# Six cross layers on one core: product 3 of layers 0 to 4 by seven half-size products, and state sums by accumulating DMAs

## The chip, the core and the metric

The kernel runs on one core of one Trainium2 chip. TensorE (PE) multiplies, ScalarE (ACT) brings results from PSUM to SBUF, VectorE (DVE) does elementwise work, SyncE (SP) issues DMAs, GpSimd (POOL) is nearly unused. The metric is device time in microseconds, the median of several runs. One execution is taken by the profiler.

## The reference

The input has 16384 rows of 1024 columns; there are six layers with a 1024 x 1024 weight and a bias each, all in bfloat16.

```python
x = x0
for l in range(L):
    proj = jnp.einsum('bd,de->be', x, ws[l]) + bs[l]
    x = x0 * proj + x
return x
```

## The kernel before, in words

**Tiling.** Rows are worked in 16 pairs of two blocks of 512 (`NB`). Everything is held transposed, features on the 128 partitions: `x0T` and the state `xst` of a pair are tiles of 128 x (2 blocks n) x (8 feature slices) x 512; four slices make a half (`half(eh)`). Pairs go in 8 groups of two (loop `s`, pairs "A" and "B"); within a group the loop runs over layers l = 0 to 5 and in each over A and B. One pass is a **step**: 96 steps, A and B alternating, so that the elementwise end of one pair's layer lies in the other pair's step. Such an end is `trail(Y)`, run in the order that the list `order` gives.

**Products.** The two blocks and the two feature halves make a 2 x 2 matrix of blocks; a layer is one Strassen-Winograd round of seven products of 512 x 512 weights on 512 columns, numbered 1 to 7. A direct product is 16 matmuls 128x128 on 512 columns (`mm`). From the second step on product 2, and in the groups after the first also product 4, is done by a second round of seven products of 256 x 256 on 256 columns (`inner`, four matmuls each, 28 in all). In layer 0 of those groups (`in3`) product 3 is too. Its inputs are differences in `ti3` (k02, k1, k3), its result is in part accumulated in PSUM with product 5 (`S53`) and in part evicted to `E3`, `e6` and added by VectorE; `ti4` and `E4`, `e5` do the same for product 4, `ti2` and `ea`, `eb` for product 2.

**VectorE in a step.** T13 (differences T[5], T[7]), then of the other pair's trail: m1 (sum times x0), s11 (`C2` plus `P5s`), a1 (plus the state); T2, T4; s4, e4 (E4 into C2); i02, i1, i3 (inputs of product 4); mC2 and aC2 (both feature slices of the second half times x0, plus the state); then `EA` and `P1s` of the own pair, j02, j1, j3 (inputs of the next step's product 2), m0 and a0 (the first quarter of the own state), and `S53` plus `U2s`. Each is in program order (`pin`). All T tiles and evicted tiles (`U2s`, `P1s`, `S53`, `ea`, `e4`) have one buffer, `C2` (name "cb") has two.

**Weights.** The combined weights are computed in group 0 (`combo`) and stored to DRAM (`Lc`). Later groups load nine tiles of 512 KB a layer through a ring of nine (`RING`); `prefetch_upto` issues these loads on SP in the steps of pair B, each once its buffer is free. The third inner weights (`w3i`, in the buffer `P2s`) are loaded for layer 0 only.

**Inputs and outputs.** `bring("A")` and `bring("B")` load the next group's inputs by two transposing DMAs each, in layers 2 and 3 of A's steps (`pending` holds them until the weights of the step are asked for). A pair that has ended is turned by a DMA transpose (`turn_pair`) and written (`write_pair`) during the next group's layer 0.

Line names in the profile: L46 is `vtt`, L52 `acopy`, L55 `abias`, L419 `mm`, L427 `inner`, L99 `prefetch_upto`, L221 the input load, L325 and L332 `turn_pair` and `write_pair`.

Of the kernel before, what the change touches and what calls it, by code (L numbers as in the profile page):

```python
# [8 lines left out]
ADD = mybir.AluOpType.add  # L9
# [8 lines left out]
def kernel(  # L18
# [26 lines left out]
    def vtt(out, in0, in1, op):  # L45
        return pin(nc.vector.tensor_tensor(out=out, in0=in0, in1=in1, op=op))  # L46

    def vcopy(out, in_):
        return pin(nc.vector.tensor_copy(out=out, in_=in_))

# [6 lines left out]
    def pool(name, bufs, **kw):  # L57
        return ctx.enter_context(tc.tile_pool(name=name, bufs=bufs, **kw))
# [2 lines left out]
    dram = pool("dram", 1, space=bass.MemoryType.DRAM)  # L61
    big = pool("big", 1)
    t_pool, ti_pool, ei_pool = pool("tp", 1), pool("tip", 1), pool("eip", 1)
    ev_pool, cb_pool, wring = pool("evp", 1), pool("cbp", 2), pool("wring", RING)
    ps = [pool(f"ps{i}", KH, space=bass.MemoryType.PSUM) for i in range(2)]

    def wtile():
# [5 lines left out]
    def evt(name):  # L73
        return ev_pool.tile([P, KH, NB], BF16, name=name)
# [88 lines left out]
    def sub_w(w, h):  # L163
        return {(i, j): w[:, 2 * i:2 * i + 2, j * h:(j + 1) * h] for i in range(2) for j in range(2)}
# [91 lines left out]
    def trail(Y, store):  # L256

        if Y is None:
            return [None] * 7
        C2, E4, e5 = Y.C2, Y.E4, Y.e5  # L260
        eh1 = lambda t: t[:, :, KH:KD, :]
        m1, a1 = fin_of(Y, Y.C12, 0, 1)
        if Y.E3 is not None:
            def m1(E3=Y.E3, e6=Y.e6, C=Y.C12, mul=m1):
                for i in range(2):
                    vtt(E3[:, 2 * i:2 * i + 2, NQ:NB], E3[:, 2 * i:2 * i + 2, (1 - i) * NQ:(2 - i) * NQ], e6[:], ADD)
                vtt(C, C, E3, ADD)
                mul()

        def s4():  # L270
            for i in range(2):
                vtt(E4[:, 2 * i:2 * i + 2, NQ:NB], E4[:, 2 * i:2 * i + 2, (1 - i) * NQ:(2 - i) * NQ], e5[:], ADD)

        def a1s():
            if a1 is not None:
                a1()
            if store:
                store_half(Y, 0)

        return [m1, lambda: vtt(C2[:, 1], C2[:, 1], Y.P5s[:], ADD), a1s,  # L280
                s4 if E4 is not None else None,
                (lambda: vtt(C2[:, 0], C2[:, 0], E4[:], ADD)) if E4 is not None else None,
                lambda: vtt(eh1(Y.xst) if Y.l == 0 else C2[:], C2[:], eh1(Y.x0T), MULT),
                None if Y.l == 0 else (lambda: vtt(eh1(Y.xst), C2[:], eh1(Y.src_in), ADD))]

    def fin_of(Y, C, eh, n):
        xs = half(eh)
        if Y.l == 0:
            return [lambda: vtt(Y.xst[:, n, xs, :], C, Y.x0T[:, n, xs, :], MULT), None]
        return [lambda: vtt(C, C, Y.x0T[:, n, xs, :], MULT),  # L290
                lambda: vtt(Y.xst[:, n, xs, :], C, Y.src_in[:, n, xs, :], ADD)]

# [35 lines left out]
    def write_pair(Y):  # L328
        with nc.allow_non_contiguous_dma(reason="256B runs"):
            for n in range(2):  # L330
                r0 = Y.pr * PR + n * NB
                pin(nc.sync.dma_start(out[r0:r0 + NB, :].rearrange("(j p) (k r) -> p k j r", p=P, r=P),  # L332
                                      Y.x0T[:, n].rearrange("p k (j r) -> p k j r", r=P)))

    for s in range(NPAIR // 2):
        for l in range(L):
            for side in ("A", "B"):
                X, Y = cur[side], prev
                first, last = step == 0, (X.pr, l) == LAST
                in2, in4 = not first, s > 0 and not (s + 1 == NPAIR // 2 and l + 1 == L)  # L340
                X.l, in3 = l, l == 0 and s > 0
                psA, psX = ps[step % 2], ps[1 - step % 2]
                step += 1
                bias = lambda eh, m, l=l: b_all[:, l * KD + eh * KH + m: l * KD + eh * KH + m + 1]
# [5 lines left out]
                def bring(who, s=s, home=home):  # L350
                    pr = 2 * (s + 1) + (who == "B")
                    new[who] = Pair(pr, bigt(home["n" + who]))
                    load_x0(pr, new[who].x0T)

                if side == "B" and s + 1 < NPAIR // 2 and l == L - 1:
                    w3i = evt("P2s")
                    pending.insert(0, lambda w=w3i: pin(nc.sync.dma_start(w[:], lc(0, 10))))
                if side == "A" and s + 1 < NPAIR // 2:
                    if l == (2 if s > 0 else L - 1):
                        pending.append(lambda: bring("A"))  # L360
                    if l == 3 and s > 0:
                        pending.append(lambda: bring("B"))

                if s + 1 == NPAIR // 2 and side == "A" and l == 2:
                    x0R = bigt(home["nA"])[:].rearrange("p n k b -> p (n k b)").rearrange("p (j d) -> p j d", d=D)
# [66 lines left out]
                def evi(dst, pt):  # L432
                    acopy(dst, pt[:].rearrange("p (m b) -> p m b", m=2))
# [20 lines left out]
                ev(P1s, pA, 0, 0)  # L454
                t2, t4 = (None, None) if first else (X.T2, X.T4)
                i02, i1, i3 = inner_t(X, lambda: X.T[4], "ti4") if in4 else [None] * 3
                X.E3 = None
                k02, k1, k3 = [None] * 3
                if in3:
                    ti3 = X.xst[:, 0, KH:KD, :].rearrange("p q (k b) -> p q k b", k=2)  # L460
                    k02, k1, k3 = inner_t(X, lambda: X.rhs(3), "ti3", ti3)
                order = (m1, s11, a1, t2, k02, s4, k1, t4, k3, e4, i02, mC2, i1, aC2, i3)
                if in3 and side == "B":
                    order = (m1, s11, a1, t2, s4, t4, e4, k02, i02, k1, k3, mC2, i1, aC2, i3)
                for f in order:
                    if f is not None:
                        f()
                if in2:
# [47 lines left out]
                    end_of(Y, False)  # L516
                    w3 = weights(3)
                    if in3:
                        wk, wr3 = w3i[:].rearrange("p k (j e) -> p k j e", e=HE), sub_w(w3, HE)
                        b3, t3 = sub4(X.rhs(3)), X.ti3  # L520
                        colx = lambda m0, j, pX=pX: (lambda m: pX[m0 + m][:, j * NQ:(j + 1) * NQ])
                        inner(colx(0, 0), wr3[1, 0], b3[1, 0], False)
                        inner(colx(0, 1), wk[:, 2], b3[1, 1], False)
                        ev(S53, pX, 0, 0)
                        mm(5, w5, pX, 3, True)
                        ev(P5s, pX, 3)
                        ev(S53, pX, 1, 0)
                        ev(P1s, pA, 3, 0)
                    else:
                        mm(3, w3, pX, 0, False)  # L530
                        mm(5, w5, pX, 3, True)
# [66 lines left out]
                if s == 0:  # L598
                    if side == "A":
                        if l > 0 and l + 1 < L:  # L600
                            alloc(l + 1)
                        if l + 1 < L:
                            load_raw(l + 1, nc.sync, (12, 4, 1, 2) if l > 0 else (12,))
                        for pid in ((5, 6, 3) if 0 < l < L - 1 else ()):
                            combo(l + 1, pid)
                        if l in (0, L - 1):
                            combo(l, 9)
                    elif l + 1 < L:
                        for pid in (5, 6, 3) if l == 0 else ():
                            combo(1, pid)  # L610
                        combo(l + 1, 7)
                        combo(l + 1, 8)
                        if l == 0:
                            combo(0, 10)
                w6 = weights(6)
                end_of(Y, True)
                if last:
# [5 lines left out]
                if in4:  # L623
# [12 lines left out]
                    ev(U2s, pA, 0)  # L636
                    if in3:
                        y1, y5 = bank(psX), bank(psX)
                        X.E3 = X.xst[:, 1, 0:KH, :]
                        X.e6 = ei_pool.tile([P, 2, NQ], BF16, name="e6")  # L640
                        e3 = sub4(X.E3)
                    inner(cols(z1), wr4[0, 0], b4[0, 0], True)
# [22 lines left out]
                    inner(cols(z1), wj[:, 3], t4[:, 2], False)  # L665
                    evi(e4[1, 0], z1)
                    for m in range(1, KH):
                        mm(7, w7, pA, m, False)
                        ev(C2[:, 1], pA, m, 1)
                        if in3 and m == 1:  # L670
                            inner(cols(y1), wk[:, 3], t3[:, 2], False)
                            evi(e3[1, 0], y1)
# [13 lines left out]
                else:  # L686
# [11 lines left out]
                if s == 0 and side == "B" and 0 < l < L - 1:  # L698
                    combo(l, 9)
                if not last:  # L700
                    vtt(S53[:], U2s[:], S53[:], ADD)
                if late:
                    for f in (j02, j1, j3):
                        if f is not None:
                            f()
# [49 lines left out]
```

## Time and profile before

| | us |
|---|---|
| median of 3 runs | 2262.93 (2262.43 to 2262.95) |
| the profiled execution | 2263.38 |
| its span, first to last instruction | 2261.6 |
| a step of group 0 (layers 1 to 5) | 23.78 |
| a step of later groups, layers 1 to 5 | 23.38 |
| a step of later groups, layer 0, A and B | 22.98 and 23.07 |

The granted clock of TensorE is 1.0 throughout. Steps are windows between the first matmuls of product 1. Instructions on VectorE overlap a little: their durations add up to more than the time that they take in a row, so spacing from start to start is what is added.

### The profile page before, as it was taken

What the parts mean: (1) busy time and instruction counts of PE and PEld (TensorE: products, weight loads), DVE (VectorE), ACT (ScalarE), POOL (GpSimd) and SP (SyncE); (2) the same over time, 40 slices, a digit from 0 to 9 for tenths busy, and PEclk for the clock granted to TensorE, in tenths of its full rate; (3) what the DMA queues carried; (4) which work ended last, traced back from release to release, by engine and by line L of the source; (5) the groups of instructions that cost most, each with busy time, mean ns of one, the idle gap of its engine ahead of it and who ended that gap; (6) DMA issues with size and microseconds to landing.
All of it is one profiled execution on the core that took longest, in us unless ns stands there. A gap on an engine that the chain in (4) does not pass through costs nothing.

```text
span 2261.6 us, 33979 instructions
## 1 busy us (share of the span) xinstructions
PE 2253.6 (100%) x13093; PEld 1279.8 (57%) x13093; DVE 2140.2 (95%) x2444; ACT 1930.2 (85%) x3363; POOL 1.6 (0%) x10
## 2 busy tenths in 40 slices
PE   9999999999999999999999999999999999999999
PEld 4555555555655556555565555655556555565554
DVE  7999989999999999999999999999999999999999
ACT  6777788888988889888898888988889888898887
POOL 0000000000000000000000000000000000000000
PEclk9999999999999999999999999999999999999999
DMA  8423595623945249543494434944348443483337
GB/s 235 156 94 121 152 212 168 148 85 125 254 136 138 89 135 250 138 127 95 137 263 122 122 110 135 250 121 121 123 132 240 121 131 122 132 231 122 104 120 177
DMA packets 509606, 338.82 MB, mean 150 GB/s; under 512 B 390658, under 2 KB 470532, under 8 KB 509444
## 3 DMA queue, kind: packets, MB, share of 16 engines
q1 hardware_dynamic: 509444, 336.65, 53.5%
q8 instruction: 103, 1.69, 0.3%
q14 instruction: 59, 0.48, 0.1%
HBM read 217.59 MB, written 52.95 MB: 120 GB/s over the span
## 4 chain that ended last, share of the span: by engine, by line
PE 99%; DMA 0%; DVE 0%; SPq 0%; issue 0%; ACT 0%; DVEq 0%
PE px L419 72%; PE px L427 26%; PE px L414 1%; DMA wp<-in_ws_dram 0%; DVE cb L46 0%; SPq L120 0%; DVE eb L46 0%; DVE T L46 0%; SPq L210 0%; PE px L411 0%; PE px L409 0%; DVE wp L46 0%; ACT cb L52 0%; SPq L213 0%; DVEq L46 0%
## 5 line engine op out<-in xcount | busy, mean ns | idle before, releaser
L419 PE MATMUL px<-T,wp 128*128 128x512 bf16 x4384 | 1071.7, 379 | 0.0
L419 PEld LDWEIGHTS <-wp 128*128 128x128 bf16 x7120 | 696.5, 98 | 637.4 <-issue 0.7
L419 PE MATMUL px<-big,wp 128*128 128x512 bf16 x2736 | 659.3, 379 | 0.4 <-ACT big L52 0.4
L427 PEld LDWEIGHTS <-wp 128*128 128x128 bf16 x4920 | 480.8, 98 | 257.4 <-DVE big L46 2.8
L55 ACT ACTIVATE cb<-px,b_all 128x512 bf16<-128x512 f32 x760 | 504.5, 689 | 78.4 <-PE px L419 64.9
L427 PE MATMUL px<-ti,wp 128*128 128x256 bf16 x2684 | 402.6, 273 | 0.0
L52 ACT CAST ea<-px 128x512 bf16<-128x512 f32 x344 | 201.7, 586 | 133.5 <-PE px L427 133.5
L46 DVE TENSOR_TENSOR T<-big 128x4096 bf16<-128x4096 bf16 (+1 forms) x97 | 220.1, 2269 | 77.9 <-PE px L419 77.2
L52 ACT CAST U2s<-px 128x512 bf16<-128x512 f32 x384 | 229.2, 597 | 55.2 <-PE px L419 52.7
L55 ACT ACTIVATE P1s<-px,b_all 128x512 bf16<-128x512 f32 x380 | 254.2, 694 | 5.7 <-PE px L419 4.2
L55 ACT ACTIVATE S<-px,b_all 128x512 bf16<-128x512 f32 x380 | 244.1, 703 | 0.8 <-PE px L419 0.8
L46 DVE TENSOR_TENSOR T<-big,T 128x2048 bf16<-128x2048 bf16 x192 | 233.9, 1218 | 1.2
L52 ACT CAST P5s<-px 128x512 bf16<-128x512 f32 x384 | 219.5, 596 | 17.3 <-PE px L419 16.1
L46 DVE TENSOR_TENSOR big<-cb,big 128x4096 bf16<-128x4096 bf16 x95 | 217.0, 2284 | 0.4
L52 ACT CAST e<-px 128x512 bf16<-128x512 f32 x342 | 204.4, 606 | 0.0
L427 PE MATMUL px<-big,wp 128*128 128x256 bf16 x1252 | 187.9, 273 | 0.0
L46 DVE TENSOR_TENSOR cb<-cb,big 128x4096 bf16<-128x4096 bf16 (+2 forms) x89 | 184.9, 2080 | 0.7 <-ACT cb L52 0.5
L52 ACT CAST eb<-px 128x512 bf16<-128x512 f32 x258 | 152.2, 590 | 6.2
L427 PE MATMUL px<-T,wp 128*128 128x256 bf16 x984 | 134.2, 273 | 0.0
L46 DVE TENSOR_TENSOR S<-U2s,S 128x2048 bf16<-128x2048 bf16 (+1 forms) x97 | 117.1, 1207 | 3.1 <-ACT U2s L52 3.0
L46 DVE TENSOR_TENSOR cb<-cb,P5s 128x2048 bf16<-128x2048 bf16 (+1 forms) x97 | 117.1, 1208 | 0.1
L46 DVE TENSOR_TENSOR P1s<-P1s,big 128x2048 bf16<-128x2048 bf16 x90 | 109.7, 1219 | 7.9 <-ACT P1s L55 7.8
(81 smaller groups left out, 1475.7 us busy)
## 6 DMA issues: line engine op xcount, KB each, us to landing
wp<-Lc SPq DMA_DIRECT2D x252, 512.0 KB, 4.7
wp<-in_ws_dram SPq DMA_DIRECT2D x144, 512.0 KB, 3.7
out_dram<-big SPq DMA_DIRECT2D x28, 1024.0 KB, 11.0
Lc<-big SPq DMA_DIRECT2D x15, 512.0 KB, 2.7
Lc<-wp SPq DMA_DIRECT2D x9, 512.0 KB, 2.7
Lc<-ti SPq DMA_DIRECT2D x7, 512.0 KB, 3.7
P2s<-Lc SPq DMA_DIRECT2D x7, 512.0 KB, 4.6
ea<-in_ws_dram SPq DMA_DIRECT2D x6, 512.0 KB, 5.0
```

The lines of the kernel that those rows point to most:

```text
L46: return pin(nc.vector.tensor_tensor(out=out, in0=in0, in1=in1, op=op))
L52: return pin(nc.scalar.copy(out=out, in_=in_))
L55: return pin(nc.scalar.activation(out=out, in_=in_, func=IDENT, bias=bias, scale=1.0))
L414: nc.tensor.matmul(pt, lhsT=rhs[:, k, m * P:(m + 1) * P], rhs=wt[:, k, :], start=(start and k == 0 and pid != 1), stop=(k == KH - 1), **kw)
L419: nc.tensor.matmul(pts[m][:], lhsT=wt[:, k, m * P:(m + 1) * P], rhs=rhs[:, k, :], start=(start and k == 0), stop=(k == KH - 1), **kw)
L427: nc.tensor.matmul(dst(m), lhsT=w[:, k, m * P:(m + 1) * P], rhs=rhs[:, k, :], start=(start and m == 0 and k == 0), stop=(k == 1), skip_gro ...
```

## The change

- `in3` holds in layers 0 to 4 of the groups after the first: product 3 by seven products there. `E3` and `ti3` get tiles of their own. The third weights are loaded once a layer (`load_third`, in B's step for the next layer), and `combo` stores them for layers 0 to 4.
- `by_dma(Y)` holds in layers 1 to 4 of pair A and 1 to 3 of pair B. There three of the four state sums become accumulating DMAs on GpSimd's queue (`dadd`, state += product): m1d from `U2s`, m2d from `C2[:, 1]`, m0 from a tile in the one buffer of T2. The fourth stays on VectorE. The DMAs write into the state in place.
- The E3 corrections and S53 += E3 move from the next step's m1 to the end of the own step; mC2 stands before i02.
- `C2` has one buffer.
- Both inputs of the next group are loaded in layer 5 of A.
- In group 0 combo 9 stands in A's steps and combo 10 in B's.

```diff
+    def dadd(out, in_):
+        pin(nc.gpsimd.dma_start(out=out, in_=in_, accum_op=ADD))
...
-    ev_pool, cb_pool, wring = pool("evp", 1), pool("cbp", 2), pool("wring", RING)
+    ev_pool, cb_pool, wring = pool("evp", 1), pool("cbp", 1), pool("wring", RING)
...
+        mul = lambda n: vtt(C2[:, n], C2[:, n], Y.x0T[:, n, KH:KD, :], MULT)
+        def m1d():
+            vtt(Y.U2s[:], Y.C12, Y.x0T[:, 1, 0:KH, :], MULT)
+            dadd(Y.xst[:, 1, 0:KH, :], Y.U2s[:])
+        def m2d():
+            mul(1)
+            dadd(Y.xst[:, 1, KH:KD, :], C2[:, 1])
+        if dma:
+            return [m1d, s11, m2d, s4, e4, lambda: mul(0),
+                    lambda: vtt(Y.xst[:, 0, KH:KD, :], Y.xst[:, 0, KH:KD, :], C2[:, 0], ADD)]
...
+    def by_dma(Y):
+        return 0 < Y.l < L - 1 - Y.pr % 2
...
+        if by_dma(Y):
+            def m0():
+                t = t_pool.tile([P, KH, NB], BF16, name="T2")
+                vtt(t[:], C, Y.x0T[:, n, xs, :], MULT)
+                dadd(Y.xst[:, n, xs, :], t[:])
+            return [m0, None]
...
+    def load_third(l):
+        third[l] = evt("P2s")
+        pin(nc.sync.dma_start(third[l][:], lc(l, 10)))
...
-                X.l, in3 = l, l == 0 and s > 0
+                X.l, in3 = l, s > 0 and l < L - 1
...
-                    if l == (2 if s > 0 else L - 1):
+                    if l == L - 1:
                         pending.append(lambda: bring("A"))
-                    if l == 3 and s > 0:
-                        pending.append(lambda: bring("B"))
+                        if s > 0:
+                            pending.append(lambda: bring("B"))
...
-                order = (m1, s11, a1, t2, k02, s4, k1, t4, k3, e4, i02, mC2, i1, aC2, i3)
-                if in3 and side == "B":
-                    order = (m1, s11, a1, t2, s4, t4, e4, k02, i02, k1, k3, mC2, i1, aC2, i3)
+                order = (m1, s11, a1, t2, s4, t4, e4, k02, k1, k3, mC2, i02, i1, i3, aC2) if in3 else (m1, s11, a1, t2, s4, t4, e4, i02, mC2, i1, aC2, i3)
...
+                        if side == "B" and l + 1 < L - 1:
+                            load_third(l + 1)
...
+                if in3:
+                    for i in range(2):
+                        vtt(X.E3[:, 2 * i:2 * i + 2, NQ:NB], X.E3[:, 2 * i:2 * i + 2, (1 - i) * NQ:(2 - i) * NQ], X.e6[:], ADD)
+                    vtt(S53[:], S53[:], X.E3[:], ADD)
```

More of the change, by code (lines that the diff above doesn't have):

```diff
@@ L261, in trail @@
         eh1 = lambda t: t[:, :, KH:KD, :]
[L262 to L268, printed above, removed]
+        dma = by_dma(Y)
+        mul = lambda n: vtt(C2[:, n], C2[:, n], Y.x0T[:, n, KH:KD, :], MULT)
         def s4():
@@ L272, in s4 @@
                 vtt(E4[:, 2 * i:2 * i + 2, NQ:NB], E4[:, 2 * i:2 * i + 2, (1 - i) * NQ:(2 - i) * NQ], e5[:], ADD)
+        def m1d():
[4 more added lines that the diff above has]
+            dadd(Y.xst[:, 1, KH:KD, :], C2[:, 1])
+        s11 = lambda: vtt(C2[:, 1], C2[:, 1], Y.P5s[:], ADD)
+        e4 = (lambda: vtt(C2[:, 0], C2[:, 0], E4[:], ADD)) if E4 is not None else None
+        if E4 is None:
+            s4 = None
+        if dma:
+            return [m1d, s11, m2d, s4, e4, lambda: mul(0),
+                    lambda: vtt(Y.xst[:, 0, KH:KD, :], Y.xst[:, 0, KH:KD, :], C2[:, 0], ADD)]
+        m1, a1 = fin_of(Y, Y.C12, 0, 1)
         def a1s():
@@ L278, in a1s @@
                 store_half(Y, 0)
-        return [m1, lambda: vtt(C2[:, 1], C2[:, 1], Y.P5s[:], ADD), a1s,
-                s4 if E4 is not None else None,
-                (lambda: vtt(C2[:, 0], C2[:, 0], E4[:], ADD)) if E4 is not None else None,
+        return [m1, s11, a1s, s4, e4,
                 lambda: vtt(eh1(Y.xst) if Y.l == 0 else C2[:], C2[:], eh1(Y.x0T), MULT),
                 None if Y.l == 0 else (lambda: vtt(eh1(Y.xst), C2[:], eh1(Y.src_in), ADD))]
+    def by_dma(Y):
+        return 0 < Y.l < L - 1 - Y.pr % 2
     def fin_of(Y, C, eh, n):
@@ L333, in write_pair @@
                                       Y.x0T[:, n].rearrange("p k (j r) -> p k j r", r=P)))
+    third = {}
+    def load_third(l):
+        third[l] = evt("P2s")
+        pin(nc.sync.dma_start(third[l][:], lc(l, 10)))
     for s in range(NPAIR // 2):
@@ L355 @@
                 if side == "B" and s + 1 < NPAIR // 2 and l == L - 1:
-                    w3i = evt("P2s")
-                    pending.insert(0, lambda w=w3i: pin(nc.sync.dma_start(w[:], lc(0, 10))))
+                    pending.insert(0, lambda: load_third(0))
                 if side == "A" and s + 1 < NPAIR // 2:
-                    if l == (2 if s > 0 else L - 1):
+                    if l == L - 1:
                         pending.append(lambda: bring("A"))
-                    if l == 3 and s > 0:
-                        pending.append(lambda: bring("B"))
+                        if s > 0:
+                            pending.append(lambda: bring("B"))
                 if s + 1 == NPAIR // 2 and side == "A" and l == 2:
@@ L456 @@
                 i02, i1, i3 = inner_t(X, lambda: X.T[4], "ti4") if in4 else [None] * 3
-                X.E3 = None
                 k02, k1, k3 = [None] * 3
                 if in3:
-                    ti3 = X.xst[:, 0, KH:KD, :].rearrange("p q (k b) -> p q k b", k=2)
-                    k02, k1, k3 = inner_t(X, lambda: X.rhs(3), "ti3", ti3)
-                order = (m1, s11, a1, t2, k02, s4, k1, t4, k3, e4, i02, mC2, i1, aC2, i3)
-                if in3 and side == "B":
-                    order = (m1, s11, a1, t2, s4, t4, e4, k02, i02, k1, k3, mC2, i1, aC2, i3)
+                    k02, k1, k3 = inner_t(X, lambda: X.rhs(3), "ti3")
+                order = (m1, s11, a1, t2, s4, t4, e4, k02, k1, k3, mC2, i02, i1, i3, aC2) if in3 else (m1, s11, a1, t2, s4, t4, e4, i02, mC2, i1, aC2, i3)
                 for f in order:
@@ L518 @@
                     if in3:
-                        wk, wr3 = w3i[:].rearrange("p k (j e) -> p k j e", e=HE), sub_w(w3, HE)
+                        wk, wr3 = third[l][:].rearrange("p k (j e) -> p k j e", e=HE), sub_w(w3, HE)
                         b3, t3 = sub4(X.rhs(3)), X.ti3
@@ L605 @@
                             combo(l + 1, pid)
-                        if l in (0, L - 1):
-                            combo(l, 9)
+                        combo(l, 9)
                     elif l + 1 < L:
@@ L612 @@
                         combo(l + 1, 8)
-                        if l == 0:
-                            combo(0, 10)
+                        combo(l, 10)
                 w6 = weights(6)
@@ L638 @@
                         y1, y5 = bank(psX), bank(psX)
-                        X.E3 = X.xst[:, 1, 0:KH, :]
+                        X.E3 = ei_pool.tile([P, KH, NB], BF16, name="e3")
                         X.e6 = ei_pool.tile([P, 2, NQ], BF16, name="e6")
@@ L664 @@
                     ev(C2[:, 1], pA, 0, 1)
-                    inner(cols(z1), wj[:, 3], t4[:, 2], False)
-                    evi(e4[1, 0], z1)
+                    if in3:
+                        inner(cols(y1), wk[:, 3], t3[:, 2], False)
+                        evi(e3[1, 0], y1)
+                        if side == "B" and l + 1 < L - 1:
+                            load_third(l + 1)
+                    else:
+                        inner(cols(z1), wj[:, 3], t4[:, 2], False)
+                        evi(e4[1, 0], z1)
                     for m in range(1, KH):
@@ L670 @@
                         if in3 and m == 1:
-                            inner(cols(y1), wk[:, 3], t3[:, 2], False)
-                            evi(e3[1, 0], y1)
+                            inner(cols(z1), wj[:, 3], t4[:, 2], False)
+                            evi(e4[1, 0], z1)
                     col = lambda m0, j, pA=pA: (lambda m: pA[m0 + m][:, j * NQ:(j + 1) * NQ])
@@ L697 @@
                         ev(C2[:, 0], pA, m, 1)
-                if s == 0 and side == "B" and 0 < l < L - 1:
-                    combo(l, 9)
+                X.U2s = U2s
                 if not last:
                     vtt(S53[:], U2s[:], S53[:], ADD)
+                if in3:
+                    for i in range(2):
+                        vtt(X.E3[:, 2 * i:2 * i + 2, NQ:NB], X.E3[:, 2 * i:2 * i + 2, (1 - i) * NQ:(2 - i) * NQ], X.e6[:], ADD)
+                    vtt(S53[:], S53[:], X.E3[:], ADD)
                 if late:
```

## The prediction

> **What bounds the kernel now.** I read the page first: the busy shares, then the chain that ended last.
>
> ```profile
> PE 2253.6 (100%) x13093; PEld 1279.8 (57%) x13093; DVE 2140.2 (95%) x2444; ACT 1930.2 (85%) x3363; POOL 1.6 (0%) x10
> ...
> PE 99%; DMA 0%; DVE 0%; SPq 0%; issue 0%; ACT 0%; DVEq 0%
> ```
>
> TensorE is the bound, almost alone; VectorE at 95% is so close behind that a busy share can't say which of them sets the time once TensorE has less to do. So next the windows view, one window a step (a step is one layer of one pair of batch blocks; there are 96), with the time, then PE, PEld, DVE and ACT busy time, granted clock, DMA share and GB/s.
>
> ```profile
> 576.03:599.01 22.98, 22.98 (x150) 14.49 (x148) 22.72 (x29) 21.44 (x40) 0.00 (x0) 1.00 1.13 270
> 599.01:622.08 23.07, 23.07 (x151) 14.38 (x148) 21.55 (x30) 21.46 (x40) 0.00 (x0) 1.00 0.95 256
> ...
> 645.46:668.84 23.38, 23.38 (x139) 13.30 (x137) 22.43 (x26) 20.10 (x36) 0.00 (x0) 1.00 0.43 144
> 668.84:692.22 23.38, 23.38 (x139) 13.32 (x137) 22.43 (x26) 20.10 (x36) 0.00 (x0) 1.00 0.66 150
> ...
> 762.36:785.74 23.38, 23.38 (x139) 13.31 (x137) 22.43 (x26) 20.11 (x36) 0.00 (x0) 1.00 0.16 62
> ```
>
> These are layers 0A, 0B, 1B, 2A and 4A of one group. Layer 0 already computes product 3 by seven small products and takes 22.98 (A) where layers 1 to 5 take 23.38: the trace holds the change's main effect as a row, 0.40 us a step. ACT's extra evictions (21.46 of 22.98) fit there. VectorE is the question: 22.43 of 23.38 now. The timeline of layer 2A gives its spacing from start to start (start, duration).
>
> ```profile
> 666.87 2.29 DVE L46 TENSOR_TENSOR T<-big 128x4096 bf16<-128x4096 bf16 x1 [0.84 <-PE px L419]
> 669.08 1.22 DVE L46 TENSOR_TENSOR S<-S,big 128x2048 bf16<-128x2048 bf16 x1
> 670.21 1.22 DVE L46 TENSOR_TENSOR cb<-cb,P5s 128x2048 bf16<-128x2048 bf16 x1
> ...
> 673.62 0.76 DVE L46 TENSOR_TENSOR e<-e,e 128x512 bf16<-128x512 bf16 x2
> 674.29 1.22 DVE L46 TENSOR_TENSOR T<-big,T 128x2048 bf16<-128x2048 bf16 x1
> ...
> 682.30 1.02 DVE L46 TENSOR_TENSOR ea<-ea,eb 128x1024 bf16<-128x1024 bf16 x2
> 683.43 1.23 DVE L46 TENSOR_TENSOR P1s<-P1s,ea 128x2048 bf16<-128x2048 bf16 x1
> ...
> 690.25 2.29 DVE L46 TENSOR_TENSOR T<-big 128x4096 bf16<-128x4096 bf16 x1 [0.84 <-PE px L419]
> ```
>
> So 4096 elements cost 2.21, 2048 cost 1.135, a pair of 512 costs 0.67 (0.335 each), the two of EA 1.13. Where an instruction reads what the one right before it wrote, the spacing is 0.12 more (two `ti<-big,ti` at 594.90 and 595.36, 0.46 apart). The only idle time is 0.84 before T13, which waits for the last matmul of product 7. TensorE in the same step:
>
> ```profile
> 667.54 1.03 PE L419 MATMUL px<-big,wp 128*128 128x512 bf16 x4
> ...
> 671.00 0.60 PE L427 MATMUL px<-ti,wp 128*128 128x256 bf16 x4
> 671.44 1.03 PE L419 MATMUL px<-big,wp 128*128 128x512 bf16 x4
> ...
> 685.29 1.89 PE L419 MATMUL px<-T,wp 128*128 128x512 bf16 x8
> ...
> 687.45 2.75 PE L419 MATMUL px<-T,wp 128*128 128x512 bf16 x12
> ```
>
> Four 512-wide matmuls take 0.864 (667.54 to 668.40), four 256-wide ones 0.44. T13 (690.25) starts right behind the twelve of 687.45, 0.67 before the next step's first matmul (690.92).
>
> **TensorE.** In layers 1 to 4 of the seven groups after the first (s = 1 to 7), 56 steps, 16 x 0.216 = 3.45 us become 28 x 0.109 = 3.05: -0.40 each, **-22.4 us**, if nothing else comes to bind. The first group (s = 0), layer 5, start and tail keep their products.
>
> **VectorE, a step of layers 1 to 4.** Removed: the sums a0, a1 (2 x 1.135), and mC2 and aC2 of 4096 (4.42). Added: mul(1), mul(0) and one sum of 2048 (3.41), k02, k1, k3 (4 x 0.335), two e3 corrections (0.67) and S53 += E3 (1.135). The step's sum is then twelve of 2048 (13.62), T13 (2.21), seventeen of 512 (5.70), 0.79 for the one of 1024: 22.3, with five dependent neighbours (mul(1), k3, i3, j3, S53 += E3, 0.6) about **22.9 against TensorE's 22.98**. This is the thin place, so I laid it along TensorE's step (0 = first matmul of product 1). T13 starts at -0.67; T2 ends at 6.2 (product 6 starts at 11.27), k3 at 10.6 (its first reader at 12.13), the first of i02 at 12.2 (reader at 13.87). m0 now writes a tile from the T2 buffer and waits for product 6's last matmul, at 17.55 where VectorE is ready at 17.3; queued behind it are j1, j3, S53, the E3 work and the next T13, which so starts at 22.55 instead of 22.31. That is 0.25 late with 3.3 us left before its reader (product 5), and does not add up, since m0's gate is TensorE's. An error of mine of 0.3 a step would grow to 2 us over the seven steps, against 1.5 us of slack before k3's reader, and is given back in layer 5 (22.43 of 23.38).
>
> Layer 0 gets the E3 work into its own step and mC2 ahead of i02. 0A sums to 24.95 in 22.98; T13 of 0B starts 2.0 late, and the first of i02 ends at about 14.0 where its reader stands at 13.87; 0B itself sums to 21.6 and catches up. So 0B, 23.07 now, I take at 23.2: 7 x 0.13 = **+1 us** (0 to 2).
>
> **The accumulating DMAs**, 168 of 512 KB, three a step. No row shows one, nor any DMA issued by GpSimd. Landing times of the DMA view:
>
> ```profile
> wp<-Lc SPq DMA_DIRECT2D x252, 512.0 KB, 4.7
> ...
> out_dram<-big SPq DMA_DIRECT2D x28, 1024.0 KB, 11.0
> Lc<-wp SPq DMA_DIRECT2D x9, 512.0 KB, 2.7
> ...
> big<-big SPq DMA_TRANSPOSE x19, 12.7
> ```
>
> Each must read two operands. Bounds: 2.7 (nearest plain copy out of SBUF) and 12.7. I take 6: a 4.7 load plus the engine time of one more (layers 4A and 1B together hold nine loads in 0.59 x 23.38 = 13.8 us, 1.5 each). Who waits: T2 of the next step for m0's DMA, ACT's first U2s eviction for m1d's, ACT's first C2 eviction for m2d's, T13 of the step after next for both. m0 ends at 18.7, T2 wants to start at 28.1 (5.1 of the next step): 9.4. m1d ends at 2.9, U2s is evicted at 12.6: 9.7, and 2 more before an inner product meets its undrained bank. m2d: 13. T13: 17. With 6 all are covered; the cost is nothing, and below 9.4 it stays nothing. As an estimate from the Trainium skill's DMA: Bandwidth & Descriptors (Anatomy of one DMA), 2.0 us plus bytes at 436 GB/s, with the bytes read twice as its Collectives: The Full Stack says of a DMA that adds (Why ReduceScatter is half of AllGather), it would be 4.4 and the sum the same; no run here shows it yet.
>
> DMA share: three of about 3 us of engine time add 0.39 to 0.16 (A) and 0.43 (B): below 1. GpSimd waits for VectorE in order, and nothing else is queued there.
>
> **Moved.** The input loads go from 2A and 3A to 5A: SP spends 11 us on each pair (10.97 at 669.40), so 22 us from 1.9 into 5A; behind them on SP stand the third-weight load and the ring loads of 5B, the first of which issues 3.65 into 5B anyway (556.30). The engines get 2 x 0.5 x 23.38 = 23.4 us of work in 5A, next to shares of 0.84, 1.13 and 0.95 in 5B, 0A and 0B. Their readers (the j work of 5B and 0A) come over 30 us later; 0A's weights have 19 us. Nothing; without that lead, every us late would cost 7. The third weights load once a layer (5 instead of 1 a group): issued some 22.5 into B, landing 4.6 later at about 4 of the next step, read at 10: nothing. combo 9 and 10 in s = 0: 4 more of 1.35 us, against 3.3 us a pair saved by the DMAs there; TensorE stays at 23.78.
>
> **Sum:** the profiled 2263.4 (span 2261.6 and 1.8 around it) - 22.4 + 1 = 2242.0; the median of the runs is 0.45 lower, so **2241.5**.
>
> **Rivals.**
> (a) *The accumulate lands late; slower.* m0 (1.135), the landing of its DMA, then VectorE's work from T2 to the next m0 (12.2 with its dependents) close a loop of 13.4 plus the landing. Above 9.6 it sets the pace instead of TensorE; above 10.0 a step is longer than the 23.38 of before. At 11.0 the step is 24.4, +1.4 in 49 steps: 2310; at 12.7 it is 26.1, 2393. For it: the rows above it in bytes and the two reads; against: share 0.16 to 0.43 in these steps.
> (b) *GpSimd cannot write descriptors while VectorE runs; much slower.* VectorE idles under 0.3 us a step in the new schedule. If descriptors get through only in such gaps, landing takes a step, 23 us or more, loop (a) goes to 36.4: +13.4 x 49, about 2900. It decides from the same 9.6. In milder form GpSimd holds VectorE up: over 0.65 us a step (gain 3.2 and slack 1.5 over seven steps) the change loses. The Trainium skill's SBUF page (Summary: rules for kernel authors) warns that descriptor generation is starved while VectorE is in a 2x or 4x mode, but under Who interferes with whom gives tensor_tensor no two-port mode. The trace shows nothing: GpSimd issues no DMA in it.
> (c) *Small waits eat part.* VectorE or ACT over by 0.3 to 0.5 a step: half the gain, 2246 to 2258, or all of it, 2259 to 2267.
> (d) The 256-wide matmuls do not pay: excluded by the rows of layer 0.
>
> **Chances.** Forecast 0.62; (c) 0.10 faster and 0.04 without change; (a) 0.16; (b) 0.08. Faster 0.72, same 0.04, slower 0.24; 0.2% (4.5 us) is about what a measurement of this kernel can tell from no change. The range starts at 2238 (no cost in 0B, 22.4 saved, and a little) and reaches into (a) at a landing of 10.7 to 2295, which leaves out the rest of (a) and (b), some 0.17. The forecast's own range is 2238 to 2246.
>
> **What would show it.** Right: windows of 22.98 in layers 1 to 4; no wait of VectorE's T or ACT's U2s and cb for a DMA; landing under 9.4; an idle of some 0.2 before `T<-P1s,big` and none before T13. Wrong: those waits in the waits view, TensorE gaps released by DVE `ti`, or durations of VectorE above 1.22 beside the new DMAs.

## The result and the profile after

The changed kernel takes **2285.72 us** (median of 4 runs, 2285.66 to 2287.02), the kernel before 2262.74 (2262.43 to 2262.95): ratio 1.0101, 95% interval 1.0089 to 1.0114. It is 23 us slower, where 21 us faster was forecast. Its profiled span is 2283.8 us at a granted clock of 0.999.

Page of the changed kernel: busy times, and the chain that ended last.

```profile
PE 2225.6 (97%) x13503; PEld 1345.2 (59%) x13765; DVE 2168.0 (95%) x2796; ACT 2020.0 (88%) x3587; POOL 146.2 (6%) x178
...
PE 85%; DVE 10%; issue 2%; ACT 1%; DMA 1%; SPq 0%; DVEq 0%; ACTq 0%
```

TensorE's share fell from 100% to 97%: it now waits. (Its busy time is 28 us less than before, a little too much: 13503 matmuls are recorded for 13765 weight loads.) The chain names ACT with 1% only and is little help in finding the wait. The windows are, for 0A, 1B and 3A of one group (time, PE, PEld, DVE, ACT and POOL busy time, granted clock, DMA share, GB/s). Each window, here and in the prediction, runs from the second block of product 1, 1.30 us behind the step's first matmul, to the same place in the next step:

```profile
578.64:602.27 23.63, 22.98 (x147) 14.47 (x148) 23.39 (x32) 21.65 (x40) 0.00 (x0) 1.00 1.12 248
649.54:673.17 23.63, 23.04 (x148) 14.48 (x148) 22.85 (x32) 21.65 (x40) 2.58 (x3) 1.00 0.77 209
720.44:744.07 23.63, 22.98 (x147) 14.44 (x148) 22.85 (x32) 21.65 (x40) 2.58 (x3) 1.00 0.61 150
```

TensorE works some 23 us, the forecast length of a step, but the step takes 23.63. All 70 steps that compute product 3 by seven small products are so, layer 0's included (only 1A of the first of the seven groups is longer, 24.00). By layers: 56 steps of layers 1 to 4 at +0.25 against before (14.0), seven of 0A at +0.65 (4.6), seven of 0B at +0.56 (3.9): 22.5, against 22.2 more of span. The list of waits names the cause.

```profile
DVE T L46 <- PE px L448: 64.6, 126, 2.4
...
PEld L456 <- issue: 53.9, 70, 0.8
...
PE px L456 <- ACT e L56: 37.3, 70, 0.7
```

Seventy times, once a step, TensorE waits for ACT to evict a tile `e`. The timeline of TensorE at the end of layer 2B shows which:

```profile
712.85 0.60 PE L456 MATMUL px<-ti,P2s 128*128 128x256 bf16 x4
713.29 1.03 PE L448 MATMUL px<-T,wp 128*128 128x512 bf16 x4
714.81 0.60 PE L456 MATMUL px<-ti,P2s 128*128 128x256 bf16 x4 [0.49 <-ACT e L56]
715.46 0.81 PE L448 MATMUL px<-T,wp 128*128 128x512 bf16 x3
```

And ACT's at the same time:

```profile
713.56 0.70 ACT L56 CAST U2s<-px 128x512 bf16<-128x512 f32 x1
714.04 0.71 ACT L56 CAST e<-px 128x512 bf16<-128x512 f32 x1
714.52 0.83 ACT L59 ACTIVATE cb<-px,b_all 128x512 bf16<-128x512 f32 x1
```

The small product at 712.85 (third weights, in tile `P2s`) adds into bank y1; ACT must evict y1 before the next small product adds into it. ACT takes the last `U2s` eviction first and has y1 out at 714.75, 1.90 after that product began. Between the two products stands one block of product 7, from 713.29 to 714.15 by the spacing of 0.864. TensorE so goes on at 714.81 instead of 714.15: 0.66 lost, which is the 0.65 of the step.

The change had turned the order here: y1's last product behind block 0 of product 7 and z1's behind block 1. Neither the list of the change above nor the lines shown of its diff name this turn; the edit of run 1 below undoes just it. The kernel before has the two the other way round in layer 0, and waits for neither. There y1's second and last product and, between them, ACT's evictions of the last `U2s` and of y1 (into `E3`, then a part of the state's tile `big`) are these, in 0A:

```profile
592.08 0.60 PE L427 MATMUL px<-big,P2s 128*128 128x256 bf16 x4
594.67 0.60 PE L427 MATMUL px<-big,P2s 128*128 128x256 bf16 x4
```

```profile
592.78 0.70 ACT L52 CAST U2s<-px 128x512 bf16<-128x512 f32 x1
593.26 0.71 ACT L52 CAST big<-px 128x512 bf16<-128x512 f32 x1
```

The eviction ends at 593.97, 1.89 after the first of the products began, and the next begins 2.59 after it.

### The profile page after: what moved, and what is told of

Its sections match the earlier page's. It is cut to its first block, busy times and chain, and to the rows that moved or that the text cites. A ratio compares the mean times of both kernels' runs of the same rounds, so it can differ in the third digit from the quotient of the medians.

```text
span 2283.8 us, 36260 instructions
## 1 busy us (share of the span) xinstructions
PE 2225.6 (97%) x13503; PEld 1345.2 (59%) x13765; DVE 2168.0 (95%) x2796; ACT 2020.0 (88%) x3587; POOL 146.2 (6%) x178
## 3 DMA queue, kind: packets, MB, share of 16 engines
q0 software_dynamic: 24192, 88.09, 20.7%
## 4 chain that ended last, share of the span: by engine, by line
PE 85%; DVE 10%; issue 2%; ACT 1%; DMA 1%; SPq 0%; DVEq 0%; ACTq 0%
PE px L448 55%; PE px L456 29%; DVE big L46 2%; DVE ti L46 2%; DVE cb L46 2%; DVE T L46 2%; ACT e L56 1%; PE px L443 1%; DVE S L46 1%; DVE ea L46 0%; DVE e L46 0%; DMA P2s<-Lc 0%; DMA wp<-in_ws_dram 0%; SPq L124 0%; DVE eb L46 0%
## 5 line engine op out<-in xcount | busy, mean ns | idle before, releaser
L448 PEld LDWEIGHTS <-wp 128*128 128x128 bf16 x6224 | 608.9, 98 | 507.7 <-issue 0.5
L456 PEld LDWEIGHTS <-wp 128*128 128x128 bf16 x5592 | 547.1, 98 | 263.9
L456 PE MATMUL px<-ti,wp 128*128 128x256 bf16 x2964 | 444.6, 273 | 0.1
L448 PE MATMUL px<-big,wp 128*128 128x512 bf16 x1760 | 439.9, 379 | 4.5 <-ACT big L56 0.4
L56 ACT CAST e<-px 128x512 bf16<-128x512 f32 x608 | 366.1, 646 | 6.6
L456 PE MATMUL px<-big,wp 128*128 128x256 bf16 x1644 | 246.6, 273 | 0.0
L46 DVE TENSOR_TENSOR cb<-cb,big 128x2048 bf16<-128x2048 bf16 (+3 forms) x145 | 193.9, 1339 | 2.6 <-ACT cb L56 0.5
L456 PE MATMUL px<-ti,P2s 128*128 128x256 bf16 x840 | 125.8, 272 | 37.3 <-ACT e L56 37.3
L456 PEld LDWEIGHTS <-P2s 128*128 128x128 bf16 x1120 | 109.1, 97 | 88.9 <-issue 53.9
L50 POOL DMA_DIRECT2D big<-T x56 | 48.3, 863 | 1571.4 <-DVE T L46 1558.2
L46 DVE TENSOR_TENSOR ti<-big,ti 128x512 bf16<-128x512 bf16 x332 | 140.2, 422 | 4.9
```

Source lines behind the costliest of these rows:

```text
L50: pin(nc.gpsimd.dma_start(out=out, in_=in_, accum_op=ADD))
L56: return pin(nc.scalar.copy(out=out, in_=in_))
L448: nc.tensor.matmul(pts[m][:], lhsT=wt[:, k, m * P:(m + 1) * P], rhs=rhs[:, k, :], start=(start and k == 0), stop=(k == KH - 1), **kw)
L456: nc.tensor.matmul(dst(m), lhsT=w[:, k, m * P:(m + 1) * P], rhs=rhs[:, k, :], start=(start and m == 0 and k == 0), stop=(k == 1), skip_gro ...
```

## The experiments

The theory: the turned order alone costs 0.65 in each of 70 steps (45.5 us), and everything else of the change does about what was forecast. Against it stand the prediction's own rivals: accumulating DMAs that land late, GpSimd and VectorE in each other's way.

**1. The changed kernel with the old order of y1 and z1.**

```
 mm(7, w7, pA, 0, False); ev(C2[:, 1], pA, 0, 1)
-if in3: inner(cols(y1), wk[:, 3], ...); evi(e3[1, 0], y1); load_third
-else:   inner(cols(z1), wj[:, 3], ...); evi(e4[1, 0], z1)
+inner(cols(z1), wj[:, 3], ...); evi(e4[1, 0], z1)
 ...  # behind block 1, in3 only:
-inner(cols(z1), wj[:, 3], ...); evi(e4[1, 0], z1)
+inner(cols(y1), wk[:, 3], ...); evi(e3[1, 0], y1); load_third
```

> Theory W: the change's step of layers 0 to 4 takes 23.63 instead of 22.98 because the last small product into bank y1 now stands only one block of product 7 (0.86 us) behind the product before it in the same bank, whose eviction by ACT needs 1.5 us; TensorE stands still for 0.65 us in 70 steps, 45.5 us. With the old order of the two (z1 first, y1 one block later) and all else as in the change, steps take 22.98 and the time is 2241 (2239 to 2244). Rival V: VectorE, at 22.9 of work a step by the prediction's sum, is the real pace and the wait only shows it; then a wait of TensorE for VectorE takes the place, steps stay at 23.4 or more and the time above 2270. Rival D: the accumulating DMAs slow ACT's evictions; then the time stays above 2255, since they are still there.

Measured: **2243.24 us** (2242.88 to 2243.44), ratio to before 0.9913 (0.9896 to 0.9929). Windows of 0B and of 3A:

```profile
595.92:619.12 23.20, 23.15 (x151) 14.40 (x149) 22.82 (x31) 21.55 (x40) 0.00 (x0) 1.00 0.91 260
711.05:734.03 22.98, 22.98 (x150) 14.48 (x148) 22.70 (x32) 21.45 (x40) 2.59 (x3) 1.00 0.60 154
```

Its TensorE timeline around the small products in question:

```profile
704.11 0.60 PE L456 MATMUL px<-ti,P2s 128*128 128x256 bf16 x4
...
706.71 0.60 PE L456 MATMUL px<-ti,P2s 128*128 128x256 bf16 x4
```

Now 2.60 us lie between the two products into y1, more than the 1.90 that the eviction needs. The wait is gone, and with it 42 us. It is not the whole 45.5, mainly because 0B has 0.2 of its own left, and in the first of the seven groups 0B and 1A 0.4 each: 2.1 in all. Both numbers of the prediction for a step stand: 22.98, and 23.20 in 0B.

**2. The kernel before with only the order turned**, in its 14 steps of layer 0; nothing else of the change.

> The kernel before, with only the order of the two small products turned round in the 14 steps of layer 0 that do product 3 by seven. No accumulating DMA, nothing else of the change. Theory W: 14 x 0.65 = 9.1 us slower, 2271.8 (2269 to 2273), layer 0 steps at 23.6. Rivals V and D: no change, 2262.7, since VectorE has no more work there and there are no such DMAs.

Measured: **2271.77 us** (2271.48 to 2272.47), ratio 1.0039 (1.0024 to 1.0054); 0A and 0B take 23.63 each, and TensorE waits 14 times for ACT to evict y1:

```profile
PE px L427 <- ACT big L52: 6.2, 14, 0.5
```

So the turn costs the same 0.6 a step where there is neither an accumulating DMA nor a new sum. Runs 1 and 2 together show the cause by taking it away and by adding it alone.

**3. The changed kernel with the places of y1's second product and of y5's exchanged**, so that y1 is out earlier and the turned order might stand.

```
-inner(cols(y5), wk[:, 0], t3[:, 0], True);  evi(X.e6[:], y5)
+inner(cols(y1), wk[:, 1], t3[:, 1], False); evi(e3[0, 1], y1)
 ...
-inner(cols(y1), wk[:, 1], t3[:, 1], False); evi(e3[0, 1], y1)
+inner(cols(y5), wk[:, 0], t3[:, 0], True);  evi(X.e6[:], y5)
```

> The change, with the places of the small products into y1 (second) and y5 exchanged: the three products into y1 then stand behind blocks 1 and 2 of product 6 and block 0 of product 7, so that each finds the bank evicted (1.3 and 2.2 us between them), and E3 is complete as early as in the change. Theory W: no wait, 2241 (2239 to 2246; up to 0.1 a step if the first eviction, behind that of e5, ends late). Rival V: above 2270. Rival D: above 2255.

Measured: **2267.45 us** (2266.7 to 2269.72), ratio 1.0019 (1.001 to 1.0029), well above what was expected. The wait was moved, not removed; TensorE's timeline, then ACT's:

```profile
708.51 0.59 PE L448 MATMUL px<-T,wp 128*128 128x512 bf16 x2
709.33 0.60 PE L456 MATMUL px<-ti,P2s 128*128 128x256 bf16 x4 [0.22 <-ACT e L56]
```

```profile
707.65 0.65 ACT L56 CAST U2s<-px 128x512 bf16<-128x512 f32 x1
708.13 1.14 ACT L56 CAST e<-px 128x512 bf16<-128x512 f32 x2
709.09 0.68 ACT L56 CAST U2s<-px 128x512 bf16<-128x512 f32 x1
```

The product now moved forward meets y1 before its first eviction is done, because that stands second in ACT's queue and ends at 709.27. In this trace the product stands in the middle of a block of product 6, two matmuls ahead of it and two behind. By starts it is 0.39 late (708.51 and half a block of 0.43 make 708.94), and steps of 23.36 follow. It is the same path at an earlier pair of products: y1's product before it began at 706.77, so that 2.50 were needed and 2.17 given. The eviction's place in ACT's queue, not its own duration, set when the bank was free.

**4. Run 1 with every sum on VectorE** (`by_dma` returns False).

> The old order of the two products as in e1, and all four state sums on VectorE again (no accumulating DMA). By the prediction's sum VectorE then has 22.9 + 3.3 = 26.2 us a step in layers 1 to 4 and sets the pace: about 49 x 3.2 above e1, less the slack of layer 5, 2370 to 2400. If the DMAs cost VectorE or ACT more than they save (rival D), the time is at or below the change's 2286.

Measured: **2381.18 us** (2381.01 to 2381.3), ratio 1.0522 (1.0507 to 1.0538). Without the DMAs VectorE is busy for up to 25.8 us a step, steps grow to 26.0, and TensorE waits for VectorE, most of all for `ti`. A window of 3B, and that wait:

```profile
761.31:787.29 25.98, 23.98 (x151) 14.32 (x149) 25.77 (x33) 21.20 (x41) 0.00 (x0) 1.00 0.39 131
```

```profile
PE px L456 <- DVE ti L46: 44.2, 47, 1.8
```

The accumulating DMAs are what makes the gain of 0.40 a step possible; they are worth 138 us against this.

**5. Run 1 with `i02` and `i1` ahead of `mC2` in 0A, 0B and 1A**, to test where 0B's 0.2 comes from.

```
-order = (..., k02, k1, k3, mC2, i02, i1, i3, aC2)
+order = (..., k02, k1, k3, i02, i1, mC2, i3, aC2)   # where Y.l is 0 or L - 1
```

> e1 with i02 and i1 ahead of mC2 in the three steps of a group whose trail still has the whole 4096-wide work (0A, 0B, 1A). The prediction's step of layer 0: in 0B, VectorE starts 2.0 late and the first of i02 ends 0.15 to 0.25 behind its reader. e1 shows 0B at 23.20 (23.39 and 1A 23.36 in the first of the seven groups). If that is the cause, 0B takes 22.98 and the time falls by 7 x 0.22 + 0.6 = 2.1 us to 2241.1 (2240.5 to 2242). Rival: 0B waits for something else, such as a late weight behind the output DMAs; then no change, 2243.2.

Measured: **2242.48 us** (2241.35 to 2244.1), ratio 0.9906 (0.9892 to 0.992), 0.5 above the range expected. Its window of 0B:

```profile
595.50:618.49 22.99, 22.99 (x151) 14.49 (x149) 22.53 (x30) 21.43 (x40) 0.00 (x0) 1.00 0.92 252
```

0B has 22.99 for 23.20, and the span 2239.5 for 2240.9: the late `i02` was the cause. The runs themselves overlap with those of run 1, so that this is the best version of these runs is shown by the profile alone.

**6 and 7. Run 1 with one, then two plain 512 KB copies by GpSimd to DRAM ahead of each accumulating DMA**, to find how late these may land (rival a) and whether GpSimd slows VectorE (rival b).

> e1 with a plain DMA of the same 512 KB to an unused place in DRAM, issued by GpSimd ahead of every accumulating DMA: doubles what GpSimd issues, and each accumulate lands some 2 us later. By the prediction's margins (T2 9.4, U2s 9.7, C2 13 us) landings of 6.6, 8 and 10 cost nothing: 2243 to 2244. If issuing DMAs on GpSimd holds VectorE up (rival b of the prediction, in its mild form), VectorE has no slack left in e1 and the time rises above 2250, with VectorE durations over 1.22.

> e1 with two such plain DMAs ahead of every accumulating one (88 to 264 MB on GpSimd's queue): each accumulate lands some 4 to 6 us later, T at 9 to 11, cb at 12 to 16, at and over the margins. By the loop of rival (a), 13.4 us plus T's landing, a landing of 10.5 makes steps of 23.9 in 49 steps and a time of 2285; waits of VectorE's T or ACT's U2s and cb for a DMA show in the trace. If the margins were wider than reckoned, 2243.

With one: **2246.43 us** (2245.33 to 2247.32), ratio 0.9923 (0.9909 to 0.9937). The accumulating DMAs land after 6.4 to 10.5 us (medians), nearly all steps stay at 22.98, and VectorE's sums stay at 1.22. The time is 3 us above run 1, and above what was expected. The profiled span is 3.7 longer, of which some 2.2 are lost by the end of the first 0A and 1.3 in one step of the last group; there ACT has to wait for accumulating DMAs to land (into `cb` 5.8 us in three waits, into `U2s` 2.7 in five), as it never does in run 1. With two: **2442.11 us** (2438.81 to 2451.91), ratio 1.0795 (1.0773 to 1.0817), far above the 2285 expected, and not through the loop of rival (a) in the first place. The waits of the run with two:

```profile
PEld L461 <- DMA P2s<-Lc: 152.6, 22, 9.6
ACT S L63 <- PE px L461: 150.3, 30, 9.3
PE px L461 <- DMA P2s<-Lc: 146.6, 21, 9.3
...
DVE T L46 <- DMA big<-T: 52.6, 21, 3.3
...
ACT cb L63 <- DMA big<-cb: 28.3, 24, 4.3
```

The third-weight load gives way most: its first reader stands 9.3 us behind its issue in the changed kernel (672.44 to 681.74), and here it lands after 14.6 (median). Rival (a)'s wait, `T` for `big<-T`, comes second, and ACT's for the DMA of `cb` third; all of it lies in the A steps of layers 2 to 4, which take 28 to 35 us, while the B steps stay near 23. Two plain DMAs beside each accumulating one are far more than the schedule bears; one is about as much as it does. Whether the weights would be late without the waits of `T` was not separated.

**8. Run 1 with the next input loaded in layers 2 and 3 again**, where the kernel before has it.

> e1 with the next group's inputs loaded in layers 2 and 3 of A again, beside the accumulating DMAs. The prediction costed this move at nothing in either place: 2243 (2242 to 2245). Rival: the input transposes (share +0.5 of the DMA engines over a step) push the accumulates past the margins there, two steps a group: up to 7 x 2 x 1.0 = 14 us more, 2250 to 2257.

Measured: **2536.4 us** (2512 to 2548), ratio 1.119 (1.1134 to 1.1246), far outside what was expected. 2A and 3A take 42 to 53 us. (In the 2A of the lines below, 47.5 us long, 2.5 of the 24.5 us more are TensorE's own work, 25.51 for 22.98, at a granted clock of 0.75.) The list of waits, and SP's queue in 2A:

```profile
ACT U2s L56 <- DMA big<-U2s: 265.6, 12, 28.6
PE px L456 <- ACT e L56: 262.4, 12, 28.3
```

```profile
723.29 0.43 SPq L363 DMA_DIRECT2D P2s<-Lc  x1
724.07 0.32 SPq L103 DMA_DIRECT2D wp<-Lc  x1
724.43 39.85 SPq L225 DMA_TRANSPOSE big<-in_x_dram  x2
```

Two transposing loads hold SP for 39.85 us instead of 10.97, and the accumulating DMA issued beside them lands after 32.6 instead of 5.6. Both are slower together than apart, and ACT's eviction into `U2s` waits for it. Which property of these DMAs does it? Four runs on the kernel before, with its sums on VectorE and its input in layers 2 and 3, add three 512 KB DMAs a step behind the sums that the change moved.

**9 and 10. Plain copies to DRAM, issued by GpSimd, then by ACT.**

> The kernel before, with its input loads where they were (layers 2 and 3 of A) and its sums on VectorE; only three plain copies of 512 KB a step to DRAM scratch are added, issued by GpSimd, where the changed kernel has its three accumulating DMAs. Nobody waits for the copies. If it is the adding (two operands, SBUF to SBUF) that does not go beside the transposing input loads, the copies land in 3 to 9 us there as elsewhere, SP's issue of two transposes in 2A stays near 11 us, and the time is 2263 to 2267. If any DMA that GpSimd issues and the transposes hold each other up, SP's issue of the pair of transposes takes 20 to 40 us, copies issued in 2A and 3A land 15 to 30 us late, the weights behind the transposes on SP come late, and the time is 2300 to 2550.

> As the run with the copies issued by GpSimd, but the same copies are issued by ACT. ACT waits in its own order for VectorE's sums before it issues, so its evictions come later and the steps of layers 1 to 5 get longer whatever the transposes do (a guess of 1 to 4 us each, 2320 to 2550). The rows that decide are in 2A and 3A: if it is a matter of bytes or packets on the shared engines, SP's issue of the transposes grows beyond 11 us here as with GpSimd; if it belongs to the queue that GpSimd issues to, it stays near 11 us and the copies land in 3 to 9 us.

GpSimd: **2264.95 us** (2263.24 to 2267.22), ratio 1.0007 (0.9996 to 1.0019). SP's pair in 2A:

```profile
670.11 12.59 SPq L229 DMA_TRANSPOSE big<-in_x_dram  x2
```

The copy issued beside it lands after 7.4 us. It is not GpSimd's queue. ACT: **2954.3 us**, ratio 1.3048 (1.3011 to 1.3086), above the range given; ACT waits 569 us for VectorE ahead of its evictions of `P1s`, since in its order the copies stand before them and wait for VectorE's sums, and TensorE waits 452 us for these evictions. SP's pair takes 12.72 there as well; the run tells no more of the transposes.

**11 and 12. Accumulating DMAs into DRAM; plain copies from SBUF to SBUF.**

> The kernel before with its input loads in layers 2 and 3 of A, and three DMAs of 512 KB a step issued by GpSimd as in the run with plain copies, but accumulating: they add the sum just made into DRAM scratch (the first twelve are plain copies that fill the scratch). Nobody waits for them. If adding itself is what does not go beside the transposing input loads, SP's pair of transposes takes 25 to 40 us here in 2A and 3A, adds issued beside them land after 20 to 33 us, and weights behind the transposes come late: 2300 to 2500. If it is writing into SBUF from GpSimd's queue, or the waits that the changed kernel hangs on it, the pair stays at 11 to 14 us and the time at 2263 to 2268, with landings of 4 to 9 us.

> The same places and sizes, but plain copies from SBUF to SBUF (each copies the quarter of the state just written onto itself, so that its readers wait for it as they wait for an accumulating DMA in the changed kernel). If writing into SBUF from GpSimd's queue beside the transposes is the cause, the pair of transposes takes 25 to 40 us, these copies land 20 to 33 us after issue in 2A and 3A, and the time is 2300 to 2550. If only adding does it, they land in 4 to 9 us, the pair stays at 11 to 14 us and the time is 2263 to 2275.

Adds into DRAM: 2340.4 and 2395.24 us in its two executions, with 2263.27 for the kernel before beside them; even the shorter is 77 us longer. The longer was profiled. SP's pair in its 2A, and its longest pair:

```profile
687.82 39.49 SPq L230 DMA_TRANSPOSE big<-in_x_dram  x2
...
1034.16 66.86 SPq L230 DMA_TRANSPOSE big<-in_x_dram  x2
```

Adds land after up to 48.4 us (median 7.1), and TensorE waits up to 46.0 us for the weights that stand behind the transposes on SP. Copies from SBUF to SBUF: **2263.2 us**, ratio 1.0002 (0.9991 to 1.0013), and its pair:

```profile
668.75 12.82 SPq L228 DMA_TRANSPOSE big<-in_x_dram  x2
```

So it is the adding, into SBUF or DRAM: beside accumulating DMAs a pair of transposing loads holds SP for 36 to 47 us (run 8) and for 16 to 67 (run 11), beside plain ones of the same size, place and queue for 11 to 14 (runs 9 and 12). Why adding does this is not shown by these runs. A rival is that an add merely takes twice the time of a copy on the DMA engines; no run has plain copies of twice the time beside the transposes. The queues speak against it, without settling it. Here are the packets of SP's queue (q1) and of GpSimd's (q0), with MB and the time that they took as a share of the 16 engines' (packets overlap a little, so a share can pass 100%): in run 8, in the 41 us from the start of the pair, and SP's in run 9, in 13 us:

```profile
q1 hardware_dynamic: 8129, 3.73, 98.2%
q0 software_dynamic: 288, 1.05, 22.2%
```

```profile
q1 hardware_dynamic: 7266, 2.90, 107.4%
```

The adds themselves take 22% of the engines. What grows is the time of SP's own packets, from 4.8 us of all engines a MB (1.074 x 13 / 2.90) to 10.8 (0.982 x 41 / 3.73).

## Why the prediction was wrong, point by point

**The step that failed** is a sentence of the opening part: "ACT's extra evictions (21.46 of 22.98) fit there." It took layer 0's row as a row of the changed step, but that row belongs to the old order of the two last small products. (The 21.46 is 0B's, of 23.07; 0A has 21.44 of 22.98, which makes no difference.) The diff turns the order, and the prediction gave the turn no term at all. It is the path between a product, ACT's queue and the next product into the same bank: 1.90 us needed and 0.06 more until the next product starts, 1.30 given by the order (0.44 for the product and 0.86 for a block). Run 2 prices it at 8.8 us for 14 steps; the 45.5 for 70 steps, less the 22.4 forecast, make the 23 measured. A share of 21.46 in 22.98 could not have shown it: it says that ACT has room, and not when. The rows for it were in the trace of before: layer 0's evictions of `U2s` and of y1, one behind the other, 1.89 in all.

That 2285.72 still lies inside the stated range, which goes up to 2295, is luck: the range went that far for accumulating DMAs that land late, rival (a), and in the trace nothing waits for one.

**TensorE, 22.4 us:** right. Run 1 has it: its steps of layers 1 to 4 take 22.98, but for one 1A of 23.36; 2243.24 against 2263.00 in its runs, and span 2240.9 against 2261.6.

**VectorE, 22.9 of 22.98:** right. In run 1 it shows no idle time from one T13 to the next and yet keeps the pace of 22.98, so that nothing is left over. Its T13 of two steps, with no idle time noted before either:

```profile
686.80 2.29 DVE L46 TENSOR_TENSOR T<-big 128x4096 bf16<-128x4096 bf16 x1
...
709.78 2.29 DVE L46 TENSOR_TENSOR T<-big 128x4096 bf16<-128x4096 bf16 x1
```

The idle of some 0.2 before m0 (`T<-P1s,big`), given as a sign, is in the changed kernel's trace, where the longer step leaves room, with another 0.33 before T13 where none was forecast; at the pace of run 1 neither is left:

```profile
713.05 1.22 DVE L46 TENSOR_TENSOR T<-P1s,big 128x2048 bf16<-128x2048 bf16 x1 [0.18 <-PE px L448]
```

**0B at 23.2:** right in size, 23.20 in run 1 (23.39 in the first of the seven groups), and in its cause, run 5. The changed kernel hides it behind the 23.63.

**Landing of the accumulating DMAs, 6 us taken:** right in that it costs nothing; the three kinds lie on both sides of 6. DMA issues of the changed kernel, with KB and median us to landing:

```profile
wp<-Lc SPq DMA_DIRECT2D x252, 512.0 KB, 5.9
...
big<-T POOLq DMA_DIRECT2D x56, 512.0 KB, 4.7
big<-U2s POOLq DMA_DIRECT2D x56, 512.0 KB, 5.3
big<-cb POOLq DMA_DIRECT2D x56, 512.0 KB, 7.9
```

The last is issued some 2.4 us behind the second, on the same queue. The estimate of 4.4 us from the Trainium skill's DMA: Bandwidth & Descriptors (Anatomy of one DMA), with the bytes counted twice, is near the first of them (4.7) and well under the third. Rival (a) did not come about: nothing waits for them. The weight loads got slower beside them, 5.9 for 4.7, within their lead.

**Rival (b):** not seen. VectorE's rows stay at 1.22 with three DMAs a step, and with six in run 6. That agrees with the Trainium skill's SBUF — State Buffer (Who interferes with whom), by which tensor_tensor has no two-port mode, rather than with the broader warning of its summary.

**Rival (c), small waits,** named ACT, but as an engine with too much work, at 0.3 to 0.5 a step. What came is a wait for one eviction's place in ACT's order, while ACT is busy for 21.65 of 23.63. The wait was 0.65, it also fell on the 14 steps of layer 0, and so it took more than the whole gain.

**The input loads, "nothing":** right for where the change puts them. In 5A all four take 20.05 us of SP in run 1 (22 were taken), and nobody waits. But the move was costed only by SP and by the engines' share. That it keeps the adds and the transposes apart, and is worth some 290 us with the adds in place (run 8 against run 1), was not seen; nor what `by_dma` does for it, which leaves the sums of layer 4's pair B, made in 5A, to VectorE.

**The third weights, "nothing":** right at the landing measured, 6.5 us (median; one of 9.7 makes TensorE wait 0.2). But 9.3 us from issue to first reader (10.5 by the places that the prediction took), less 6.5, is the thinnest of the DMA margins, and the prediction reckoned it with a landing of 4.6, of a load without the accumulating DMAs beside it. In run 7 it breaks most.

## What to carry to other kernels

A row of the trace prices a step only if it has the same order, and not merely the same work: where products share a bank with an eviction between them, lay out product, the evictions queued ahead on ACT, and the eviction itself against the TensorE work in between (here 1.90 needed; 2.60 costs nothing, 1.30 costs 0.65 a step; and 2.50 needed at another pair, where 2.17 costs 0.39). Sums can be moved off a full VectorE by accumulating DMAs at 5 to 8 us each, worth 138 us here, if each has its reader later than that and no transposing load is in flight beside them.

## What the runs showed of the hardware that was not expected

- An accumulating DMA of 512 KB beside transposing loads: landing 32.6 us instead of 5.6, and the pair of transposes 39.85 instead of 10.97 (run 8). The same into DRAM (16 to 67, run 11). Plain copies by GpSimd in the same places: 11.4 to 14.1 for the pair (runs 9 and 12), and 7.4 for the copy beside it.
- An accumulating DMA costs the DMA engines about twice a plain copy of its size: in the changed kernel GpSimd's queue takes 20.7% of the span of 16 engines for 88.09 MB, against 9.9% for plain copies from SBUF to SBUF (run 12).
- A GpSimd instruction that issues an accumulating DMA lasts 0.86 us, that of a plain copy 0.53 (runs 8 and 9).
